# Loading part of w4 in transfers of 112, 8 and 8 partitions in a one-core decode block

## The chip, the cores and the metric

The kernel runs on one core of a Trainium2 chip. The metric is the device time of one execution in microseconds (us); of several runs the median is given. The profile is that of one execution, with a time of its own.

## The reference, cut to what matters

x has 4 rows of 512 numbers (B = 4, one new token each), the caches hold 32 heads of 4096 positions with 128 numbers each, and everything is float32.

```python
xn = layernorm(x)
# part A: attention over a cache
q  = (xn @ wq) as (B, 32 heads, 1, 128)
s  = einsum("bhqd,bhkd->bhqk", q, k_cache) * 128**-0.5
o  = einsum("bhqk,bhkd->bhqd", softmax(s), v_cache)
A  = o as (B, 1, 4096) @ wo                           # wo: 4096 x 512
# part B: with one position the shifted token mixing gives zero, so x1 = xn
h2 = gelu(layernorm(x1) @ w3) @ w4                    # w3: 512 x 1792, w4: 1792 x 512
out = x + A + (xn + h2)
```

The two caches are 512 MiB of the 561 MB that are read. Each number of them is used once.

## The kernel before, in words

**Tiling.** The 128 pairs of batch and head are taken in 32 groups of four (`NG = 32`, `HG = 4`). The keys of one group fill one buffer of 128 partitions by 64 KB, and so do its values. There are three such buffers: `S0` and `S1` take the keys by turns, `S2` the values. Scores are worked out on VectorE (a product with the query and a sum over 128 numbers, lines 343 to 347), the exponentials on ScalarE (line 245), and the weighted sum over the values on TensorE (32 products into four column quarters of one PSUM bank).

**The load queue.** SyncE's queue (SP) issues nearly all loads, in the order of the program: wq, then keys and values by turns in a loop (lines 133 to 145), and behind the loop w3, the first rows of w4, the last group's values in two parts, the rest of w4, and wo in six pieces. SP waits in between, because a buffer has to be free: at line 149 for TensorE to have gone through the first 12 of the 32 slices of group 30's values (`v_half`), then for the rest of them (`v_free`), and at line 154 for VectorE to have finished with the last keys (`k_free`). w3 and w4 lie in `S1`, wo goes into `S0`.

**The tail.** TensorE takes the last group's values in two parts (`GF = 12` of 32 slices each time it has them), then the 14 products with w4 (line 215, behind a wait on the semaphore `s_w4`), then a transposing product that gives `X`, the attention's output with the 4096 numbers spread over 128 partitions by 32 chunks. Each chunk c of wo is 128 rows (one on each partition) by 512 columns. wo comes in pieces of 14, 8, 5, 3, 1 and 1 chunks (`PIECES`). Chunks below `CUT` are used in **wide** products: one product of 512 columns, which goes to one of four column quarters of the TensorE array, so that four chunks run side by side; their sums stand in the PSUM bank `y` and must be moved (ScalarE's copy at line 389) and folded into `total` by four products with `sel` behind the piece that ends at `SUM = 30`. Chunks from `CUT` on are used in **narrow** products: four products of 128 columns each, straight into `total`. Behind the last chunk VectorE and ScalarE copy `total` out, and two DMAs store the result. In the profile each product stands twice, since float32 goes through the array in two passes: 14 wide chunks are 28 matmuls.

**Rows and engines.** A transfer is spread over the core's 16 DMA engines. A transfer of 128 partitions gives eight rows (partitions) to each. Before the change every load but that of x (4 rows, from ScalarE's queue) has 128 partitions.

## Time and profile before

| what | value |
|---|---|
| median of 3 runs | 1304.77 us (1304.59 to 1304.85) |
| the profiled execution's own time | 1304.81 us |
| its span, first to last instruction | 1303.0 us |
| VectorE busy | 1167.6 us (90%) |
| TensorE busy | 368.5 us (28%) |
| ScalarE busy | 107.5 us (8%) |
| read from HBM | 561.00 MB, 431 GB/s over the span |

1304.81 - 1303.0 = 1.8 us lie outside the span. The views that are quoted below are: the page's lines on DMA; the chain of waits (the work that ended last, followed back); the timeline (start, duration, engine, line, operation, and in brackets the idle time before it and what ended it); stretches (busy time of each engine in a stretch, then the granted TensorE clock, the mean busy share of the 16 DMA engines and GB/s); and the DMA view of a stretch, which counts the packets that *start* in it, by size and by queue. PE is TensorE, PEld its weight load, DVE VectorE, ACT ScalarE, SPq SyncE's queue. A wait of the kind "<-PEq" or "<-issue" names no engine: it is a semaphore that the profile could not ascribe.

### The profile page before, as it was taken

The numbers are of one execution on the slowest core, as the hardware profiler recorded it, in microseconds if no ns is written. First come the engines' busy times: TensorE is split into PE (matmuls) and PEld (weight loads), VectorE is DVE, ScalarE is ACT, GpSimd is POOL, SyncE is SP. The second block draws the span as 40 slices with busy tenths as digits, with TensorE's granted clock in tenths as the row PEclk, the third lists the DMA queues.
The fourth block names the chain that finished last, engine by engine and source line by source line (L and its number), as shares of the span: only waits on it lengthen the run. The fifth ranks groups of instructions, "written<-read, shape, count | busy, mean of one in ns | idle before, by whom it ended". The sixth has DMA issues, their size and how long they took to land. (4 is left out here: it accounts for less than half of the span.)

```text
span 1303.0 us, 7123 instructions
## 1 busy us (share of the span) xinstructions
PE 368.5 (28%) x2608; PEld 130.8 (10%) x2608; DVE 1167.6 (90%) x337; ACT 107.5 (8%) x330; POOL 2.5 (0%) x10
## 2 busy tenths in 40 slices
PE   3032123333113323212333212333311333321356
PEld 1010001111001111001111000111000111100112
DVE  4999999999999999999999999999999999999970
ACT  0000000000000000000000000000000000000010
POOL 0000000000000000000000000000000000000000
PEclk9565566666566666566666556666556666655678
DMA  9999999999999999999999999999999999999998
GB/s 402 436 449 420 447 422 445 422 441 429 431 439 422 447 420 449 420 449 420 449 420 447 420 441 429 431 439 422 447 420 449 420 449 420 449 420 447 420 434 341
DMA packets 11115, 561.05 MB, mean 431 GB/s; under 512 B 1244, under 2 KB 1252, under 8 KB 1640
## 3 DMA queue, kind: packets, MB, share of 16 engines
q1 hardware_dynamic: 11096, 561.00, 99.6%
q8 instruction: 2, 0.03, 0.0%
q14 instruction: 1, 0.01, 0.0%
q10 hardware_dynamic: 16, 0.01, 0.0%
HBM read 561.00 MB, written 0.01 MB: 431 GB/s over the span
## 5 line engine op out<-in xcount | busy, mean ns | idle before, releaser
L108 PE MATMUL ps<-slot,pw 128*32 128x512 f32 x2112 | 307.7, 747 | 908.5 <-PEq L71 908.5
L347 DVE TENSOR_REDUCE sc<-slot 128x128 f32<-128x16384 f32 x32 | 551.0, 17220 | 4.2
L343 DVE TENSOR_TENSOR slot<-slot,qb 128x8192 f32<-128x8192 f32 x32 | 278.1, 8692 | 59.1 <-DVEq L71 58.5
L345 DVE TENSOR_TENSOR slot<-slot,qb 128x8192 f32<-128x8192 f32 x32 | 277.9, 8684 | 1.1 <-DVEq L71 1.1
L108 PEld LDWEIGHTS ps<-slot,pw 128*32 128x32 f32 x2112 | 84.4, 133 | 1105.4 <-issue 1105.4
L233 ACT COPY os<-ps 128x512 f32<-128x512 f32 x33 | 19.3, 585 | 895.4 <-ACTq L71 895.4
L245 ACT ACTIVATE pw<-sc,st 32x128 f32<-32x128 f32 x128 | 67.4, 526 | 214.2 <-ACTq L71 213.1
L108 PE MATMUL ps<-sel,os 128*128 128x4 f32 x264 | 33.9, 252 | 18.6 <-PEq L71 18.6
L108 PEld LDWEIGHTS ps<-sel,os 128*128 128x128 f32 x264 | 31.9, 191 | 20.6 <-issue 20.6
L245 ACT ACTIVATION_READ_ACCUMULATOR pw<-sc,st 32x1 f32 x128 | 23.5, 184 | 0.0
L364 DVE RECIPROCAL rec<-OS 128x128 f32<-128x128 f32 x1 | 1.0, 953 | 15.1 <-DVEq L71 15.1
L349 DVE TENSOR_REDUCE st<-sc 128x1 f32<-128x128 f32 x32 | 9.2, 286 | 4.7
L108 PE MATMUL ps<-rs,ones 128*128 128x4 f32 x66 | 12.7, 263 | 0.0
L108 PEld LDWEIGHTS ps<-rs,ones 128*128 128x128 f32 x66 | 9.8, 188 | 27.7 <-issue 27.7
L391 DVE COPY res<-ps 64x128 f32<-64x128 f32 x1 | 0.3, 282 | 13.1 <-PE ps L108 13.1
L337 DVE COPY qx<-Q 128x128 f32 x32 | 7.3, 227 | 5.1 <-issue 4.7
L340 DVE STREAM_TRANSPOSE qb<-qx 128x128 f32<-128x128 f32 x32 | 10.0, 312 | 1.1
L108 PE MATMUL ps<-slot,X 128*4 128x512 f32 (+1 forms) x94 | 9.0, 457 | 4.3 <-DMA slot<-in_A_wo_dram 4.3
L253 ACT COPY OS<-ps 128x8 f32 x32 | 5.3, 165 | 43.8 <-ACTq L71 43.8
L326 DVE MEMSET pw<- 128x256 f32 x1 | 0.3, 272 | 8.7 <-DVEq L71 8.7
L351 DVE STREAM_TRANSPOSE mt<-mx 128x32 f32<-128x32 f32 x32 | 6.8, 212 | 1.1
L352 DVE TENSOR_REDUCE st<-mt 128x1 f32<-128x32 f32 x32 | 5.9, 186 | 1.1
(57 smaller groups left out, 44.9 us busy)
## 6 DMA issues: line engine op xcount, KB each, us to landing
slot<-in_A_k_cache_dram SPq DMA_DIRECT2D x2, 4096.0 KB, 36.5
slot<-in_A_wq_dram SPq DMA_DIRECT2D x1, 5120.0 KB, 22.6
slot<-in_A_v_cache_dram SPq DMA_DIRECT2D x1, 5120.0 KB, 21.0
slot<-in_B_w_dram SPq DMA_DIRECT2D x1, 3584.0 KB
slot<-in_A_wo_dram SPq DMA_DIRECT2D x1, 3584.0 KB, 29.4
slot<-in_A_wq_dram SPq DMA_DIRECT2D x1, 3072.0 KB, 11.0
slot<-in_A_v_cache_dram SPq DMA_DIRECT2D x1, 3072.0 KB, 13.5
slot<-in_B_w_dram SPq DMA_DIRECT2D x1, 2560.0 KB, 26.7
```

The lines of the kernel that those rows point to most:

```text
L108: return e.matmul(o, l, r, start=start, stop=stop)
L233: return e.copy(os[:, :, :], pv[:, :].rearrange("p (m d) -> p m d", m=4)).then_inc(a_p, 1)
L245: i = e.activation(o, sc[r, :].rearrange("p (a w t) -> p a t w", w=4, t=4), AF.Exp, bias=st[r, 1:2], scale=1.0, accum_out=rs[r, h:h + 1])
L253: return e.copy(o, oz[:, 0:2 * HG].unsqueeze(1))
L337: own(e.tensor_copy(qx[:, :].rearrange("p (h r) -> p h r", h=4), Q[:, bass.ds(g + n, 1), :].rearrange("p o h -> p (o h)").unsqueeze(2) .to ...
L340: own(e.transpose(qb[:, :], qx[:, :]))
L343: mark(e.tensor_tensor(out=K[:, :C // 2, :], in0=K[:, :C // 2, :], in1=qw, op=ALU.mult))
L345: own(e.tensor_tensor(out=K[:, C // 2:, :], in0=K[:, C // 2:, :], in1=qw, op=ALU.mult))
L347: mark(e.reduce_sum(sc[:, :], K, axis=AX.X))
L349: own(e.reduce_max(st[:, 0:1], sc[:, :], axis=AX.X))
L351: own(e.transpose(mt[:, :], mx[:, :]))
L352: e.tensor_reduce(st[:, 1:2], mt[:, :], axis=AX.X, op=ALU.max, negate=True).then_inc(d_a, 1)
```

## The change

The first part of w4 has six of 14 blocks of 512 columns (12 KB on each partition) where it had four (8 KB). It is no longer one transfer of 128 partitions but three: partitions 0 to 111, 112 to 119 and 120 to 127, with a semaphore increment each, so that TensorE waits for 64 in place of 32. The rest of w4 has eight blocks where it had ten. Chunk 26 of wo moves from the wide products to the narrow ones (`CUT` 27 to 26).

```diff
-    CUT = 27
+    CUT = 26
+    W4A = 6
...
-            e.dma_start(w4_sb[:, 0:4, :], w4_r[:, 0:4, :]).then_inc(s_w4, 16)
+            for p0, p1 in ((0, 112), (112, 120), (120, P)):
+                e.dma_start(w4_sb[p0:p1, 0:W4A, :], w4_r[p0:p1, 0:W4A, :]).then_inc(s_w4, 16)
             e.wait_ge(v_half, NG)
             e.dma_start(S2[:, FIRST], vf[NG - 1][:, FIRST]).then_inc(s_v, 16)
             take(e, v_free)
             e.dma_start(S2[:, REST], vf[NG - 1][:, REST]).then_inc(s_q, 16)
-            e.dma_start(w4_sb[:, 4:NF, :], w4_r[:, 4:NF, :]).then_inc(s_w4, 16)
+            e.dma_start(w4_sb[:, W4A:NF, :], w4_r[:, W4A:NF, :]).then_inc(s_w4, 16)
...
-            e.wait_ge(s_w4, 32)
+            e.wait_ge(s_w4, 64)
```

On SP's queue, before, behind the loop (a row is a line of the kernel, the operation, out and in, partitions by elements; `slot` stands for all three buffers, `in_B_w_dram` is w3 or w4):

```order
L146 DMA slot<-in_B_w_dram 128x7168
L148 DMA slot<-in_B_w_dram 128x2048
L150 DMA slot<-in_A_v_cache_dram 128x6144
L152 DMA slot<-in_A_v_cache_dram 128x10240
L153 DMA slot<-in_B_w_dram 128x5120
L157 DMA slot<-in_A_wo_dram 128x7168
```

The same place of the changed kernel:

```order
L147 DMA slot<-in_B_w_dram 128x7168
L150 DMA slot<-in_B_w_dram 112x3072
L150 DMA slot<-in_B_w_dram 8x3072 x2
L152 DMA slot<-in_A_v_cache_dram 128x6144
L154 DMA slot<-in_A_v_cache_dram 128x10240
L155 DMA slot<-in_B_w_dram 128x4096
L159 DMA slot<-in_A_wo_dram 128x7168
```

One transfer has become three, ahead of the last group's values, and 1,024 elements a partition have moved from behind those values to ahead of them. What stands behind is in the same order.

On TensorE, before, the products of the end (each row counts products, not passes; `slot` is wo here):

```order
L108 MATMUL ps<-Xt,perm 128x128
L111 UNCONDITIONAL_BRANCH x2
L424 UNCONDITIONAL_BRANCH
L108 MATMUL ps<-slot,X 4x512 x27
L108 MATMUL ps<-slot,X 4x128 x12
L108 MATMUL ps<-os,sel 4x128 x4
L108 MATMUL ps<-slot,X 4x128 x8
```

The same place of the changed kernel:

```order
L109 MATMUL ps<-Xt,perm 128x128
L112 UNCONDITIONAL_BRANCH x2
L426 UNCONDITIONAL_BRANCH
L109 MATMUL ps<-slot,X 4x512 x26
L109 MATMUL ps<-slot,X 4x128 x16
L109 MATMUL ps<-os,sel 4x128 x4
L109 MATMUL ps<-slot,X 4x128 x8
```

One wide product has become four narrow ones, ahead of the four with `sel`.

## The prediction

> **What bounds the kernel now.** First the page's lines on DMA.

> ```profile
> span 1303.0 us, 7123 instructions
> q1 hardware_dynamic: 11096, 561.00, 99.6%
> HBM read 561.00 MB, written 0.01 MB: 431 GB/s over the span
> ```

> SP's queue (q1) keeps the 16 DMA engines busy for 99.6% of the span at 431 GB/s, 26.9 GB/s for each. Nothing but the loads counts until the last of them; the question is when the last row lands, and what runs behind it. Next the chain of waits, its last steps (start, us, what):

> ```profile
> 1259.76 36.56 DMA slot<-in_A_wo_dram
> ...
> 1296.36 1.88 PE ps L108 x10
> 1298.24 0.01 issue
> 1298.25 1.73 PE ps L108 x48
> ...
> 1300.00 0.28 DVE res L391
> ```

> By the chain TensorE ends the kernel alone from 1296.36 on. The timeline of the same stretch says otherwise:

> ```profile
> 1288.37 3.61 PE L108 MATMUL ps<-slot,X 128*4 128x512 f32 x28 [1.82 <-DMA slot<-in_A_wo_dram]
> 1293.28 1.91 PE L108 MATMUL ps<-slot,X 128*4 128x512 f32 x16 [1.30 <-DMA slot<-in_A_wo_dram]
> 1296.36 2.73 PE L108 MATMUL ps<-slot,X 128*4 128x512 f32 x34 [1.18 <-DMA slot<-in_A_wo_dram]
> 1298.25 0.55 PEld L108 LDWEIGHTS ps<-slot,X 128*4 128x4 f32 x24 [0.94 <-DMA slot<-in_A_wo_dram]
> 1298.28 0.58 ACT L389 COPY os<-ps 128x512 f32<-128x512 f32 x1 [15.67 <-PE ps L108]
> 1298.92 0.11 PEld L108 LDWEIGHTS ps<-os,sel 128*4 128x4 f32 x8
> 1299.03 0.22 PEld L108 LDWEIGHTS ps<-slot,X 128*4 128x4 f32 x8
> 1299.53 0.12 PEld L108 LDWEIGHTS ps<-slot,X 128*4 128x4 f32 x8 [0.28 <-DMA slot<-in_A_wo_dram]
> ```

> Each piece of wo is waited for, the last too: its weights load at 1299.53 after 0.28 us of idle time. So a transfer sets the end, and from 1299.53 a fixed tail follows. Which part of the transfer is late, the stretches tell (DMA share and GB/s stand last):

> ```profile
> 1297.00:1297.50 0.50, 0.50 (x5) 0.09 (x1) 0.00 (x0) 0.00 (x0) 0.00 (x0) 1.00 0.92 340
> 1297.50:1298.00 0.50, 0.50 (x2) 0.00 (x0) 0.00 (x0) 0.00 (x0) 0.00 (x0) 1.00 0.23 86
> 1298.00:1298.50 0.50, 0.49 (x13) 0.24 (x16) 0.00 (x0) 0.22 (x1) 0.00 (x0) 1.00 0.06 25
> 1298.50:1299.00 0.50, 0.50 (x28) 0.38 (x20) 0.00 (x0) 0.37 (x1) 0.00 (x0) 1.00 0.06 25
> ```

> A share of 0.06 is one engine of 16, and 25 GB/s its rate: from 1298.0 on **one late engine** works alone. The DMA view of single stretches shows it. Each engine closes its part of a transfer with a packet under 512 B, so a stretch with 15 of them holds all engines but one. Starts of packets in 1296.7 to 1298.0, in 1299.0 to 1299.1, in mid-run 602.4 to 603.2, and in 604.1 to 604.3:

> ```profile
> DMA packets 184, 0.33 MB, mean 255 GB/s; under 512 B 30, under 2 KB 30, under 8 KB 184
> ...
> DMA packets 1, 0.00 MB, mean 0 GB/s; under 512 B 1, under 2 KB 1, under 8 KB 1
> ...
> DMA packets 30, 0.98 MB, mean 1229 GB/s; under 512 B 15, under 2 KB 15, under 8 KB 15
> ...
> DMA packets 2, 0.07 MB, mean 328 GB/s; under 512 B 1, under 2 KB 1, under 8 KB 1
> ```

> The last two pieces have been closed by 15 engines (30 marks) by 1298.0, and the 16th closes the last at 1299.0 to 1299.1, 0.5 us before TensorE uses it (1299.53). It was as late in the middle of the run: 604.2 against 602.8, 1.4 us. The lag is constant, so it is not a slower engine but one that lost time once. Where, the queues of the stretch 2.0 to 3.9 suggest:

> ```profile
> q8 instruction: 1, 0.02, 3.8%
> ```

> A fetch of instructions (3.8% of 16 x 1.9 us = 1.16 us) sits on one engine as the loads begin. Nothing evens it out, since every load gives each engine eight rows.

> **The change part by part.** *The split.* 112 rows are seven for each engine, and eight rows are one for each of eight engines, so engines 0 to 7 carry 7 + 1 + 1 = 9 rows, 8 to 15 carry 7. A row of six blocks is 12,288 B, at 26.9 GB/s 0.456 us. Engines 8 to 15 end 0.456 us earlier, engines 0 to 7 as much later, and no later load takes it back. If the late engine is in 8 to 15, the last piece closes 0.456 us earlier; the others had closed by 1298.0, over 1.0 us before the late one, so 0.456 + 0.456 = 0.91 us still leaves it the last: the whole 0.456 us is gained. If it is in 0 to 7, they are lost.

> Which? ScalarE's load of x has four rows, on four engines. It shows in the stretch 5.5 to 6.4 (below) as four packets. The late engine's rows start at 5.10 (stretch 5.10 to 5.11) and at 10.57 (10.57 to 10.58):

> ```profile
> DMA packets 1, 0.02 MB, mean 2458 GB/s; under 512 B 0, under 2 KB 0, under 8 KB 0
> q1 hardware_dynamic: 1, 0.02, 570.0%
> ...
> DMA packets 1, 0.02 MB, mean 2458 GB/s; under 512 B 0, under 2 KB 0, under 8 KB 0
> q1 hardware_dynamic: 1, 0.02, 576.2%
> ```

> That is six rows in 5.47 us. 570% of 16 x 0.01 us is 0.912 us for one row, 5.47 us for six: no room for a packet of x. If few rows fill the lowest engines, which the change itself takes for granted, x went to 0 to 3, the late engine is one of the other twelve, and eight of those are 8 to 15: two to one.

> *Six blocks in place of four* bring 4,096 B a partition forward. Eight rows of it are 8 x 4,096 / 26.9 = 1.22 us ahead of the last values, and 1.22 us less behind them, so wo moves by nothing. SP issued w4 long before it waits for `v_half`:

> ```profile
> 1220.96 0.43 SPq L148 DMA_DIRECT2D slot<-in_B_w_dram  x1
> 1248.12 0.33 SPq L150 DMA_DIRECT2D slot<-in_A_v_cache_dram  x1
> ```

> Two more issues of 0.43 us lie in the 26.7 us between. A gap would be filled if the queue ran dry before the values come; w4's marks (1252.0 to 1252.75; 1253.75 to 1253.9) say it doesn't:

> ```profile
> DMA packets 38, 0.43 MB, mean 568 GB/s; under 512 B 14, under 2 KB 14, under 8 KB 14
> ...
> DMA packets 3, 0.05 MB, mean 328 GB/s; under 512 B 1, under 2 KB 1, under 8 KB 1
> ```

> w4 runs until 1252 and later, 4 us after the issue. No gain there. The values come later: the late engine, with seven rows of 0.456 in place of eight of 0.304 us, by 0.76 us, engines 0 to 7 by 9 x 0.456 - 8 x 0.304 = 1.67 us. Who waits for them:

> ```profile
> 1262.28 0.18 ACT L245 ACTIVATION_READ_ACCUMULATOR pw<-sc,st 32x1 f32 x1
> 1262.61 5.20 PE L108 MATMUL ps<-slot,pw 128*32 128x512 f32 x24 [5.21 <-PEq L71]
> 1274.00 6.34 PE L108 MATMUL ps<-slot,pw 128*32 128x512 f32 x40 [6.20 <-PEq L71]
> 1286.59 0.29 DVE L368 COPY X<-ps 128x128 f32<-128x128 f32 x1 [2.19 <-PE ps L108]
> ```

> The first part starts right behind the exponentials, and if its values were late, 6.20 us of idle time follow it. Those end with the second part's values: the second part starts 0.76 us later, and with it the w4 products and `X`, ready at 1286.88 + 0.76 = 1287.64. The first piece of wo is then there at 1288.37 - 0.46 = 1287.91. The cover is 0.27 us, and the 1.30 us of idle time before the second piece behind it. With 1.67 us (late engine low) `X` comes at 1288.55 and wo at 1288.83. Cost nothing; without the cover up to 1.67 - 1.30 = 0.4 us.

> *The wait for 64* stands where the wait for 32 stood, and the two small transfers end long before. Nothing.

> *Chunk 26.* The five wide chunks took 1.88 us: two rounds of four quarters at 0.865 and 0.15 at the end (3.61 us are four rounds and the same 0.15). With four chunks it is one round, 1.02 us, and four narrow products, a third of the 0.67 us that three chunks take (1298.25 to 1298.92), 0.22. The third piece is done in 1.24 us instead of 1.88, and `y`'s copy starts 0.86 us sooner. The next piece is waited for anyway, so it gains nothing. Bounds: if the 1298.25 is TensorE's and not the DMA's, still at most the slack of 0.28 us before the last piece moves.

> *Sum:* 1304.81 - 0.46 = 1304.35 for the profiled execution, 0.04 above the median: 1304.3.

> [...] The row first: x's four packets, stretch 5.5 to 6.4.

> ```profile
> q10 hardware_dynamic: 4, 0.01, 2.3%
> ```

> 2.3% of 16 x 0.9 us is 0.33 us, 83 ns for each 2 KB row, against 76 ns at an engine's full rate: four neighbouring partitions written by four engines, and no one slowed. [...]

> **The rivals.**

> *B, the late engine is one of 4 to 7.* Then the end moves the other way by the same row: 1304.77 + 0.46 = 1305.2. For it: four of twelve. Against it: eight of twelve.

> *C, rows of neighbouring partitions go in line.* In every load so far an engine has its own eight rows of 128; in the small transfers eight engines write eight neighbouring partitions at once. If g of them go in line, a row costs g x 0.456 us, and two rows add (g - 1) x 0.91 us to engines 0 to 7: 0.91 for g = 2, 2.74 for g = 4, 6.4 for g = 8. Those engines have 1.0 - 0.46 = 0.54 us in hand before they become the last, so it decides from g = 2. The end is then 0.4, 2.2 or 5.9 us later than before; I take the middle, g = 4: 1304.8 + 2.2 = 1307.0. For it: no such transfer in the trace. Against it: the 83 ns.

> *D, 112 rows are not seven each.* With eight rows on 14 engines, 0 to 7 carry ten and 14 and 15 none; the others stay. A late engine in 8 to 13 then sets the end as before: 1304.8.

> **How the numbers follow.** D, against what the change says of itself, gets 0.05, and C, for which only the 83 ns of small rows speak against, 0.15. The other 0.8 go two to one: A 0.55, B 0.25. The median's runs spread by 0.26 us, so A with its unknowns reaches from 1304.0 to 1304.7 and B with uncovered time to 1305.6. 1304.0 to 1305.6 holds A, B and D, 0.85, less their edges. A measurement of this kernel can tell about 0.2%, 2.6 us: A, B, D and C up to g = 4 are no change, C with more lines, or on top of B, is slower. Faster 0.01, same 0.92, slower 0.07.

> **What would show it.** In the profile after: in mid-run the lag of one engine as before; in wo's marks the 15 engines in two heaps, one 0.9 us behind the other, and the late engine's last mark at 1298.6 (A) or 1299.5 (B) instead of 1299.0 to 1299.1; the last weight load at 1299.07 (A) or 1299.99 (B); `X` before the first piece. Wrong: w4's rows of 12 KB that take over 0.5 us (C), or an engine that has no row in the 112 (D), or a last piece for which TensorE doesn't wait.

## The result, and the profile after

The changed kernel took 1309.32 us (median of 7 runs, 1308.28 to 1309.76) against 1304.62 for the kernel before (7 runs, 1304.40 to 1304.95): ratio 1.0034, 95% interval 1.0023 to 1.0046. That is 4.7 us slower, outside the predicted range, and slower by more than 0.2%.

The page of the changed kernel, and the end of its chain of waits:

```profile
span 1307.6 us, 7137 instructions
q1 hardware_dynamic: 11112, 561.00, 99.6%
HBM read 561.00 MB, written 0.01 MB: 429 GB/s over the span
```

```profile
1259.80 42.98 DMA slot<-in_A_wo_dram
1302.78 0.04 issue
1302.82 1.70 PE ps L109 x48
1304.52 0.02 issue
1304.55 0.28 DVE res L393
```

The DMA engines are as busy as before (99.6%), the same bytes took 4.6 us longer, and the wait for wo is where it shows: it ends at 1302.78. The share of time in which the queue was busy says nothing of this loss, the rate does. The timeline of the changed kernel, in the places that were quoted of the one before:

```profile
1279.76 7.41 PE L109 MATMUL ps<-slot,pw 128*32 128x512 f32 x40 [7.19 <-PEq L71]
1293.42 0.29 DVE L370 COPY X<-ps 128x128 f32<-128x128 f32 x1 [2.19 <-PE ps L109]
1294.80 5.32 PE L109 MATMUL ps<-slot,X 128*4 128x512 f32 x44 [1.42 <-SPq L372]
1300.93 1.27 PE L109 MATMUL ps<-slot,X 128*4 128x512 f32 x16 [0.80 <-DMA slot<-in_A_wo_dram]
1302.04 0.58 ACT L391 COPY os<-ps 128x512 f32<-128x512 f32 x1 [12.60 <-PE ps L109]
1302.82 0.55 PEld L109 LDWEIGHTS ps<-slot,X 128*4 128x4 f32 x24 [0.92 <-DMA slot<-in_A_wo_dram]
1304.07 0.12 PEld L109 LDWEIGHTS ps<-slot,X 128*4 128x4 f32 x8 [0.26 <-DMA slot<-in_A_wo_dram]
```

The second part of the last group's values already comes 5.8 us later than before (1279.76 against 1274.00), and everything behind it follows: the loss lies ahead of those values. About 1.0 to 1.2 us of the 5.8 are the two blocks of w4 that now stand ahead of them: without the split it starts at 1275.04 (experiment 1 below), with a split by columns at 1275.23 (experiment 3). `y`'s copy now ends 0.2 us before the next piece is there, which is what moving chunk 26 did, and it gains nothing. The last weight load is at 1304.07, where 1299.07 was forecast. Stretches of two us from the start of w4's first rows on (columns as above; the last two are the DMA share and GB/s), first of the changed kernel:

```profile
1250.00:1252.00 2.00, 2.00 (x24) 0.58 (x20) 2.00 (x1) 0.00 (x0) 0.00 (x0) 1.00 0.98 252
1252.00:1254.00 2.00, 1.44 (x15) 0.77 (x7) 2.00 (x1) 0.58 (x1) 0.00 (x0) 1.00 1.02 252
1254.00:1256.00 2.00, 2.00 (x22) 1.04 (x25) 2.00 (x1) 0.17 (x1) 0.00 (x0) 1.00 1.54 258
1256.00:1258.00 2.00, 1.73 (x20) 0.39 (x12) 2.00 (x1) 0.00 (x0) 0.00 (x0) 1.00 0.86 129
1258.00:1260.00 2.00, 0.00 (x0) 0.00 (x0) 1.19 (x5) 0.43 (x2) 0.00 (x0) 1.00 0.76 246
```

and of the kernel before:

```profile
1250.00:1252.00 2.00, 2.00 (x24) 0.53 (x16) 2.00 (x1) 0.00 (x0) 0.00 (x0) 1.00 1.06 444
1252.00:1254.00 2.00, 1.44 (x13) 1.09 (x10) 2.00 (x1) 0.58 (x1) 0.00 (x0) 1.00 1.02 434
1254.00:1256.00 2.00, 2.00 (x23) 0.85 (x26) 2.00 (x1) 0.17 (x1) 0.00 (x0) 1.00 1.12 479
```

With a DMA share of about one in the mean, the engines moved 252, 252, 258, 129 and 246 GB/s, 227 in the mean over 10 us, where the run's mean before is 431. By these numbers 10 x (1 - 227 / 431) = 4.7 us are lost here, an estimate that covers the whole difference. Packets were open on the engines and moved little.

How the 16 engines stand at the last pieces of wo, by packets started in 1302.0 to 1303.3 and in 1303.4 to 1303.6 of the changed kernel:

```profile
DMA packets 141, 0.24 MB, mean 186 GB/s; under 512 B 23, under 2 KB 23, under 8 KB 141
...
DMA packets 2, 0.00 MB, mean 10 GB/s; under 512 B 1, under 2 KB 1, under 8 KB 2
```

The closing marks (packets under 512 B, one for each engine and transfer) now spread over more than a us, and the last, at 1303.53, comes 0.3 us behind the one before it. In the kernel before it came 1.1 us behind (1299.03 against 1297.89). One late engine behind 15 that have long finished is no longer there, and the two heaps that the prediction named don't show either. Probably the stretch of slow loads mixed the engines.

### The profile page after: what moved, and what is told of

Same layout as the page of the kernel before. It is cut to its first block, busy times and chain, and to the rows that moved or that the text cites. A ratio compares the mean times of both kernels' runs of the same rounds, so it can differ in the third digit from the quotient of the medians.

```text
span 1307.6 us, 7137 instructions
## 1 busy us (share of the span) xinstructions
PE 364.1 (28%) x2614; PEld 129.7 (10%) x2614; DVE 1167.5 (89%) x337; ACT 107.5 (8%) x330; POOL 2.5 (0%) x10
## 3 DMA queue, kind: packets, MB, share of 16 engines
q1 hardware_dynamic: 11112, 561.00, 99.6%
HBM read 561.00 MB, written 0.01 MB: 429 GB/s over the span
## 5 line engine op out<-in xcount | busy, mean ns | idle before, releaser
L109 PE MATMUL ps<-slot,pw 128*32 128x512 f32 x2112 | 304.1, 739 | 918.9 <-PEq L71 918.9
L247 ACT ACTIVATION_READ_ACCUMULATOR pw<-sc,st 32x1 f32 x128 | 23.5, 184 | 0.0
L352 DVE COPY mx<-st 128x32 f32<-128x32 f32 x32 | 5.8, 181 | 1.1
```

Of the source, the lines that this page charges most:

```text
L109: return e.matmul(o, l, r, start=start, stop=stop)
L247: i = e.activation(o, sc[r, :].rearrange("p (a w t) -> p a t w", w=4, t=4), AF.Exp, bias=st[r, 1:2], scale=1.0, accum_out=rs[r, h:h + 1])
L352: own(e.tensor_copy(mx[:, :], st[:, 0:1].to_broadcast([P, 32])))
```

## The experiments

**Theories.** *Lines* (rival C, made wider): the rows of a transfer that is not spread over all 128 partitions fall behind ways into SBUF (the core's memory that the buffers lie in) that other engines use as well, and a way takes about one engine's rate. That is the author's supposition: no view shows a way, and which partitions and which engine belong to one is supposed as well. *Balance*: only the sum of bytes of each engine counts (the forecast). *Shape*: more transfers, or one of 112 rows, are slow whatever the partitions. *Order*: six blocks ahead of the values, or chunk 26, cost the time. Medians stand beside those of the kernel before on the same chip.

**1. No split.**

```diff
-            for p0, p1 in ((0, 112), (112, 120), (120, P)):
+            for p0, p1 in ((0, P),):
...
-            e.wait_ge(s_w4, 64)
+            e.wait_ge(s_w4, 32)
```

> The changed kernel with w4's first six blocks in one transfer of 128 partitions; chunk 26 narrow as in the change. Four theories. Lines (rows of neighbouring partitions share one way into SBUF of about one engine's rate, and only a 128-row transfer gives each engine rows behind a way of its own): 0.0 against before, within 0.3 us. Balance (the late engine is low, nothing else): 0.0. Shape (three transfers, or 112 rows, are slow to make, whatever the partitions): 0.0. Order (six blocks ahead of the values, or chunk 26 narrow, cost the time): +4.7 us, as the change.

1304.63 against 1304.56 us, ratio 1.0000 (0.9991 to 1.0010). Order falls: six blocks and 26 chunks cost and gain nothing that can be told.

**2. The split alone, with four blocks and 27 wide chunks.**

```diff
-    CUT = 26
-    W4A = 6
+    CUT = 27
+    W4A = 4
```

> The split alone: 112, 8 and 8 partitions, but four blocks (rows of 8 KB) and 27 wide chunks as before. Lines: the loss goes with the row, two thirds of 4.7: +3.1 us. Balance: +0.3 us. Shape: +4.7 us, as many transfers as in the change. Order: 0.0.

1308.05 against 1304.56 us, ratio 1.0026 (1.0016 to 1.0035): +3.5 us, three quarters of the change's loss with two thirds of its bytes. The split is the cause, and the loss grows with the row (3.5 us with rows of 8 KB, 4.7 with 12 KB).

**3. Three transfers, cut by columns.**

```diff
-            for p0, p1 in ((0, 112), (112, 120), (120, P)):
-                e.dma_start(w4_sb[p0:p1, 0:W4A, :], w4_r[p0:p1, 0:W4A, :]).then_inc(s_w4, 16)
+            for m0, m1 in ((0, 4), (4, 5), (5, W4A)):
+                e.dma_start(w4_sb[:, m0:m1, :], w4_r[:, m0:m1, :]).then_inc(s_w4, 16)
```

> The changed kernel with three transfers that each have 128 partitions (blocks 0 to 3, 4, 5). Lines: 0.0 within 0.3 us, each engine writes behind its own way. Balance: 0.0. Shape by the number of transfers: +4.7 us; shape by the 112 alone: 0.0. Order: +4.7 us.

1304.74 against 1304.56 us, ratio 1.0000 (0.9990 to 1.0010). Three transfers cost nothing that can be told where each has 128 partitions.

**4. 112 and 16 partitions**, by estimate seven rows and one for every engine (in the changed kernel each transfer of eight rows was closed by eight marks).

```diff
-            for p0, p1 in ((0, 112), (112, 120), (120, P)):
+            for p0, p1 in ((0, 112), (112, P)):
...
-            e.wait_ge(s_w4, 64)
+            e.wait_ge(s_w4, 48)
```

> The changed kernel with two transfers, 112 and 16 partitions: seven rows and one row for each engine, so no engine has more than another. Balance: 0.0. Lines: about +4 us, since the 112 rows are as in the change and the 16 rows go four to a way. Shape by number: +3 us; by the 112: +4.7 us. Order: +4.7 us.

1309.32 against 1304.56 us, ratio 1.0033 (1.0022 to 1.0044): +4.8 us, as the change. The uneven load isn't needed for the loss, so balance falls as its cause.

**5. 64 and 64 partitions.**

```diff
-            for p0, p1 in ((0, 112), (112, 120), (120, P)):
+            for p0, p1 in ((0, 64), (64, P)):
...
-            e.wait_ge(s_w4, 64)
+            e.wait_ge(s_w4, 48)
```

> The changed kernel with two transfers of 64 partitions: four rows for each engine in each, both powers of two. Balance: 0.0. Shape: 0 to +2 us (one transfer more, no odd number). Lines: in each half 16 engines write to 64 partitions, two engines to a way, so each half takes as long as 128 rows, 3.65 us, and the six blocks 7.3 in place of 3.65: +3 to +3.7 us.

1309.25 against 1304.51 us, ratio 1.0036 (1.0022 to 1.0050): +4.7 us, more than the expected 3.0 to 3.7, though the interval (2.9 to 6.5 us) reaches them. The rate is what lines gave. Stretches of this kernel:

```profile
1250.00:1252.00 2.00, 2.00 (x24) 0.54 (x16) 2.00 (x1) 0.00 (x0) 0.00 (x0) 1.00 1.05 217
1252.00:1254.00 2.00, 1.44 (x14) 1.11 (x10) 2.00 (x1) 0.58 (x1) 0.00 (x0) 1.00 0.95 209
1254.00:1256.00 2.00, 2.00 (x23) 0.83 (x26) 2.00 (x1) 0.17 (x1) 0.00 (x0) 1.00 1.03 215
```

With 16 engines busy, 209 to 217 GB/s are half of 431: these two transfers of 64 partitions went at half the rate. No odd number is involved here, so shape by the 112 falls as well.

**6 to 8. The disputed cost by itself.** Eight rows of 24 KB are loaded additionally, behind wq, into space that is free then, in the kernel *before*. Only the partitions that they go to differ, not the bytes or the source.

```diff
-    s_kh, s_h = sem("skh"), sem("sh")
+    s_kh, s_h, s_sp = sem("skh"), sem("sh"), sem("ssp")
...
+            e.dma_start(S0[0:32:4, 8192:14336], wq_r[0:8, 0:6144]).then_inc(s_sp, 16)
...
             e.wait_ge(d_T, 1)
+            e.wait_ge(s_sp, 16)
             load_k(1, 1)
```

This is f_own; g_foreign has `S0[64:96:4, ...]`, h_neigh `S0[0:8, ...]`.

> Before, with one load more behind wq, into space that is free then: eight rows of 24 KB (0.91 us each at one engine's rate) on partitions 0, 4, 8 to 28. If eight rows go to engines 0 to 7, and four neighbouring partitions are one way, each of them writes behind its own way. Lines and balance alike: engines 0 to 7 are 0.91 us later in all further loads, and the others stay. The end: 0.0 if the late engine is one of 8 to 15 (the others have 1.0 us in hand), +0.91 us if it is one of 0 to 7. Lines with other ways than four neighbouring partitions: more than +1.5 us.

> As f_own, but on partitions 64, 68 to 92: the ways of engines 8 to 15. Balance (engines alone count): the same as f_own. Lines: each of engines 8 to 15 is held up by the row that another engine writes behind its way, 0.91 us, and engines 0 to 7 take twice the time for their row, 1.8 us; so all 16 are later, and the end moves by +0.9 us if the late engine is one of 8 to 15, by +1.8 us if it is one of 0 to 7.

> As f_own, but on the neighbouring partitions 0 to 7. Balance: the same as f_own. Lines: four engines and the stream of one go behind each of two ways, a row takes 4 to 5 x 0.91 us, so engines 0 to 7 are 2.7 to 3.7 us later, and the end moves by +1.7 to +3.7 us.

f_own: 1304.84 us, ratio 1.0005 (0.9995 to 1.0014), no difference that can be told. g_foreign: 1306.16 us, 1.0013 (1.0003 to 1.0022), +1.6 us, where lines gave +0.9 (the interval, 0.4 to 2.9 us, reaches it). h_neigh: 1307.91 us, 1.0027 (1.0017 to 1.0038), +3.4 us, all against 1304.51. The same 197 KB cost nothing that can be told, 1.6 and 3.4 us by where they land. The rates of the stretches 22 to 24 and 24 to 26, first of f_own:

```profile
22.00:24.00 2.00, 0.00 (x0) 0.00 (x0) 1.09 (x4) 0.00 (x0) 0.00 (x0) 1.00 1.04 447
24.00:26.00 2.00, 1.83 (x12) 0.60 (x16) 0.00 (x0) 0.00 (x0) 0.00 (x0) 0.54 1.18 508
```

of g_foreign:

```profile
22.00:24.00 2.00, 0.19 (x4) 0.00 (x0) 1.15 (x4) 0.00 (x0) 0.00 (x0) 1.00 1.16 315
24.00:26.00 2.00, 0.37 (x4) 0.23 (x8) 0.00 (x0) 0.00 (x0) 0.00 (x0) 0.84 0.97 377
```

and of h_neigh:

```profile
22.00:24.00 2.00, 0.20 (x4) 0.00 (x0) 1.05 (x4) 0.00 (x0) 0.00 (x0) 1.00 1.63 266
24.00:26.00 2.00, 0.00 (x0) 0.00 (x0) 0.00 (x0) 0.00 (x0) 0.00 (x0) 1.00 0.63 180
```

f_own also says where the late engine is. Packets of f_own started in 21.9 to 22.6, 22.6 to 23.3 and 23.3 to 23.5:

```profile
DMA packets 30, 0.43 MB, mean 609 GB/s; under 512 B 15, under 2 KB 15, under 8 KB 15
...
DMA packets 18, 0.33 MB, mean 468 GB/s; under 512 B 8, under 2 KB 8, under 8 KB 8
...
DMA packets 6, 0.16 MB, mean 819 GB/s; under 512 B 1, under 2 KB 1, under 8 KB 1
```

15 engines close wq; then, one row later, eight close the extra row; only then does the 16th close wq, which stands ahead of the extra row in its order. The packet that ends there is a row of wq of 40 KB, open since 21.89, and a row of keys follows it. So the late engine got none of the eight rows: it is not one of the engines that take eight-row transfers, as forecast A had it. In g_foreign it gets none either (its mark is at 24.29, its row of keys starts at 24.30). That speaks against a rival that is not among the theories, that each row goes to the engine whose own way it needs: if the partitions of f_own and of g_foreign lie behind all 16 ways, the late engine would then have had a row in one of the two. Its row of 40 KB takes 1.52 us in the kernel before and 1.51 in f_own, but 2.43 in g_foreign: 0.91 more, one row of 24 KB at an engine's rate.

**9 and 10. Which partitions share a way.** As f_own, with `S0[0:128:16, ...]` and `S0[0:16:2, ...]`.

> As f_own, but the eight rows on partitions 0, 16, 32 to 112, as far from each other as eight can be. Lines of neighbours only (each way is a block of neighbouring partitions): no row meets another, each meets at most one engine's stream: 0 to +0.9 us. [...]

> As f_own, but the eight rows on partitions 0, 2, 4 to 14: two in each block of four neighbours, beside the stream of that block's engine. Lines by blocks of four: a row takes 2 to 3 x 0.91 us, +0.9 to +1.8 us, between f_own and h_neigh. If only partitions side by side disturb each other: 0.0 as f_own.

Both cost more than expected: i_step16 1307.22 us, ratio 1.0019 (1.0009 to 1.0029), j_step2 1307.08 us, 1.0016 (1.0007 to 1.0026), against 1304.60; +2.6 us in place of at most 0.9, and the interval begins at 1.2; +2.5 us in place of at most 1.8, which the interval (from 0.9 us on) still reaches. That the farthest rows cost as much as near ones rules out ways of neighbours only, and partitions 0, 4 to 28 cost nothing that can be told (0.3 us, f_own). Which partitions go together was not shown: no run here separates every pair.

**11 and 12. Why x's load showed nothing.** k_small cuts h_neigh's load into twelve transfers of 2 KB rows; l_four has four rows of 24 KB on partitions 0 to 3.

```diff
-            e.dma_start(S0[0:8, 8192:14336], wq_r[0:8, 0:6144]).then_inc(s_sp, 16)
+            for c in range(12):
+                e.dma_start(S0[0:8, 8192 + 512 * c:8704 + 512 * c], wq_r[0:8, 512 * c:512 * c + 512]).then_inc(s_sp, 16)
...
-            e.wait_ge(s_sp, 16)
+            e.wait_ge(s_sp, 192)
```

> As h_neigh, with the same bytes to the same eight partitions in twelve transfers of 2 KB rows, the row size of x's load. It asks why x's four packets took no longer than alone. If small rows slip in between (a row is short enough to be taken up ahead of the way): engines 0 to 7 are 12 x 0.08 = 1 us later and no more, the end moves by 0.0 to +0.4 us. Lines, whatever the row: as h_neigh, +3 to +3.5 us; x's load then went unhindered only because its four rows came one after another.

> As h_neigh, with four rows of 24 KB on partitions 0 to 3, the shape of x's load with rows twelve times as long. Balance: 0.0. Lines by blocks of four: four engines and one stream behind one way, five rows of 0.91 us in line, so that each of the four is about 3 us later: +1.5 to +3 us with only half of h_neigh's bytes. If four rows of one transfer don't disturb each other, as x's: 0.0.

k_small: 1307.93 us, ratio 1.0027 (1.0017 to 1.0037), +3.4, as h_neigh. l_four: 1307.20 us, 1.0020 (1.0010 to 1.0030), +2.6 with half of h_neigh's bytes, both against 1304.56. The rows of 2 KB didn't slip through, and four neighbours were enough. The stretches 22 to 24 and 24 to 26 of k_small:

```profile
22.00:24.00 2.00, 0.00 (x0) 0.00 (x0) 0.99 (x4) 0.00 (x0) 0.00 (x0) 0.77 1.46 223
24.00:26.00 2.00, 0.00 (x0) 0.00 (x0) 0.00 (x0) 0.00 (x0) 0.00 (x0) 0.50 1.04 236
```

## Why the prediction was wrong

- **What bounds the kernel: right.** The last transfer's closing marks set the end, and in the changed kernel too TensorE waits for the last piece (0.26 us of idle time at 1304.07).
- **The late engine: right.** It is late by more than a us (1.06 us at the end of wq, 1.4 in mid-run, 1.1 at the end), and f_own shows that it is not among the engines that take eight rows. B falls with that. That those are the engines 0 to 7 was the author's supposition: no view numbers the engines.
- **The step that failed** is the first of the split: "Engines 8 to 15 end 0.456 us earlier, engines 0 to 7 as much later". It priced a row by its bytes and its engine alone. In these runs a row's cost hung on the partition that it was written to (nothing that can be told, +1.6 and +3.4 us in experiments 6 to 8): in f_own the price holds (eight closing marks about 0.9 us behind the others, no change of the end), in g_foreign, with the same rows and bytes, it doesn't. In the changed kernel the rows of all three transfers were slow, the 112 included (rival C below): the loads ran at 227 GB/s for 10 us, and in place of the 0.456 us of gain stand 4.7 us of loss.
- **Why the gain could not come.** By lines, w4 lays as many rows behind each way as before, whichever engine brings them. g_foreign shows that rows which other engines write can cost an engine time: the late engine had no row more there, and lost 0.91 us on one packet (2.43 in place of 1.52 us). That the same took the gain in the changed kernel is the author's estimate and wasn't tried alone.
- **Rival C: right in kind, too small and too unlikely.** It put the line into the two transfers of eight rows and had +2.2 us for g = 4. The 112 rows are slow as well: in experiment 4 by estimate no engine has a row more than another, and the loss is the same (4.8 us). The changed kernel shows it directly. Packets started in 1249.9 to 1254.5, before a row of the two small transfers started:

```profile
DMA packets 102, 1.19 MB, mean 259 GB/s; under 512 B 5, under 2 KB 5, under 8 KB 5
q1 hardware_dynamic: 102, 1.19, 101.4%
```

Five are marks, the other 97 are rows of 12 KB of the 112, and 101.4% of 16 x 4.6 us are 74.6 us: 0.77 us for a row that was priced at 0.456. That is the sign that the prediction named for C (over 0.5 us). Seven such rows are 5.4 us in place of 3.2, so by this estimate about 2.2 us of the loss, nearly half, fall on the 112 rows, which C too had put at nothing. C had a chance of 0.15 because x's packets took 83 ns beside 76. That row was read for more than it holds: x's four rows came one after another, over 5.5 to 6.4 us. k_small shows that rows of that size do cost time when eight engines write them at once (+3.4 us).
- **Rival D: no.** The three transfers are closed by 32 marks (1254.5 to 1259.3), 16 + 8 + 8: every engine has a part of the 112 rows.
- **Six blocks, the wait for 64, chunk 26: right in that they cost nothing.** Experiment 1 has the six blocks and chunk 26 without the split, experiment 3 has the wait for 64 as well, and both ratios are 1.0000. But the cover for `X` did not hold. The prediction set the end of `X`'s copy beside the start of the first products with wo; they start 1.09 us behind it where `X` comes last: 1289.95 behind 1288.86 in experiment 1, 1289.43 behind 1288.34 in experiment 3, 1294.80 behind 1293.42 + 0.29 = 1293.71 in the changed kernel, where the last mark of wo's first piece stands at 1292.38. What caught the delay is the second cover that the prediction named, the idle time ahead of the second piece: 1.30 us before, 0.25 left in experiment 3.

What stays open is the size. Lines by ways alone give h_neigh a delay for engines 0 to 7 only, but in its stretch 23.0 to 23.8 no engine starts a packet (first h_neigh, then the kernel before):

```profile
DMA packets 0, 0.00 MB, mean 0 GB/s; under 512 B 0, under 2 KB 0, under 8 KB 0
```

```profile
DMA packets 17, 0.52 MB, mean 655 GB/s; under 512 B 1, under 2 KB 1, under 8 KB 1
q1 hardware_dynamic: 17, 0.52, 151.7%
```

Where 17 packets start otherwise, none starts in 0.8 us. The engines are not at rest, they have packets open that take long (2.9 us each in the next stretch, where f_own has 1.1). Packets started in 21.9 to 22.6, first of h_neigh, then of f_own:

```profile
q1 hardware_dynamic: 31, 0.47, 418.5%
```

```profile
q1 hardware_dynamic: 30, 0.43, 142.2%
```

In each 15 are marks. In h_neigh the other 16 take 418.5% of 16 x 0.7 us together, 2.9 us each, in f_own the other 15 take 1.1 us each. The late engine, which has none of the eight rows, needs 4.13 us for its row of 40 KB where it took 1.52 before: 2.6 us, about what the profiled execution lost (a span of 1305.5 against 1303.0). So eight rows held up an engine that had none of them. How, the runs don't tell; it may be why experiments 5, 9 and 10 came out above what lines gave.

## What to carry to other kernels

Here a load's price was set by the partitions that it writes as much as by its bytes: splitting 128 partitions into 112, 8 and 8, or into halves, cost 4.7 us for 1.6 MB of w4, splitting the same load by columns cost nothing that can be told (0.2 us). Where the DMA engines bound the kernel, as here (99.6%), try large transfers at 128 partitions first, and look at GB/s by stretch, since in experiment 5 the busy share stayed at 0.95 to 1.05 with 209 to 217 GB/s, half of 431. In g_foreign the late engine lost 0.91 us to rows that it did not carry, so giving rows of a late engine to another need not help it.
